# Key and value loads cut in two halves, and a new order of all engines, in a gated delta-rule attention kernel on one core

## The chip, the cores and the metric

The kernel runs on one core of a Trainium2 chip. Five engines work side by side, each through its own queue in order: PE (TensorE, matrix products into PSUM banks), DVE (VectorE), ACT (ScalarE), POOL (GpSimd), and SP (SyncE), which here issues every transfer (DMA). The metric is the device time of one execution in microseconds, lower is better. The time of before is the median of three runs.

## The reference

The input is four batches of eight heads, 768 tokens, 48 features per head. First a recurrence over tokens keeps a 48 x 48 state per head; then its output, 384 features per token, goes through a causal convolution gate and two products.

```python
def _attn_ref(q, k, v, beta):
    B, H, S, D = q.shape                       # 4, 8, 768, 48
    k_n = k / (np.linalg.norm(k, axis=-1, keepdims=True) + 1e-06)
    state = np.zeros((B, H, D, D), dtype=np.float32)
    for t in range(S):
        kt, vt, bt = (k_n[:, :, t], v[:, :, t], beta[:, :, t, None])
        y[:, :, t] = np.einsum('bhd,bhde->bhe', q[:, :, t], state)
        v_old = np.einsum('bhde,bhd->bhe', state, kt)
        state = state + bt[:, :, :, None] * np.einsum('bhd,bhe->bhde', kt, vt - v_old)
    return y

def _moe_ref(x, w_val, conv_w, w_out):         # x: (4, 768, 384)
    xp = np.concatenate([np.zeros((B, K - 1, D)), x], axis=1)
    for k in range(K):                         # K = 5
        gate_pre += conv_w[k][None, None, :] * xp[:, k:k + S, :]
    gate = 1.0 / (1.0 + np.exp(-gate_pre))
    return gate * (x @ w_val) @ w_out
```

## The kernel before

The 768 tokens are cut into twelve chunks of 64 (`ch` 0 to 11), two chunks to a group (`g` 0 to 5). All 32 head-and-batch pairs of a chunk lie in one tile in two halves of eight slots each (`h` 0 and 1, `HB` = 8).

Per group, `grams` loads keys by feature (`load_k`, tile KF, a part of KQ) and queries (`load_q`, tile R, also in KQ), multiplies keys with keys and queries (`kp`, `qp` in group 0, `kq` after it), and `prep` turns the key products into the coefficients of a triangular inverse. `prep` is a long row of small DVE steps: a transposition of GL into TLP (`trans_in`, L463), the norms and coefficients, rows and merges, then three transpositions out (`trans_out`, L520 and L523, the last writing XA). In every group but the first it begins with four small transfers inside GL (`realign`). Masked products go to KQ and AQ by DVE (L415).

Per chunk, `solve` finishes the inverse on PE with ACT between the steps: `m16` (out of XA), `m32` (YS), `lev1`, `lev2` (ZS), and six copies by ACT into XX. Then `chain` is the recurrence: `e` (state times keys), `eadd` on DVE (L631), `u` (XX times VT), six copies by ACT into Y and US, `s` (products with KT, keys by token, into the two banks SPS), four copies by ACT from SPS into the next chunk's Y (`sevac`), and so on to `e` of the next chunk. `y` gives the chunk's output, which ACT and twelve small transfers per group (X<-YSB) put in X. Chunk `ch` needs the state of chunk `ch - 1`, so this chain is serial over the chunks.

Per group, `moe` runs the convolution (ACT, then `tap` on DVE, L682), the sigmoid (`sig`, ACT, L686), the rounding of X into XH and XL, the products `val` (PE, L702), the gate (DVE, L707) and `outp` (PE, L712), and the stores. The weights are turned out of a 64-bit form on the way in by ACT, DVE and POOL (L299 to L318).

`Plan.add` records every step with what it reads and writes. The steps run in the order of a table of numbers, `ORDER`, which the program walks once; each engine then has its own steps in that order. `BANKS` says which of six PSUM banks a product takes. An entry of -1 in `ORDER` is `keep_warm` (L975): two matmuls of 128 x 128 zeros added to SPS, on PE alone, whose result changes nothing. Waits between engines and for transfers come from what the built instructions read and write. Transfers take eight semaphores in turn, and SP issues one only when the transfer eight places before it has landed.

Copies by ACT have line L228, the small products L243, transfers L233.

## Time and profile before

| | us |
|---|---|
| median of 3 runs | 310.89 (309.6 to 311.41) |
| the profiled execution, whole | 311.53 |
| its span, first to last instruction | 309.8 |
| PE busy | 276.2 |
| DVE busy | 230.5 |
| ACT busy | 205.7 |
| `keep_warm` on PE (L975) | 33.6 |

The span is what lies between the first and the last instruction; 1.7 us of the execution lie around it. A busy time is the sum over the span of the stretches in which the engine works on something. PE's busy time contains the `keep_warm` products, which are no work of the reference. The times of the rows further down run from the span's start.

### The profile page before, as it was taken

Reading aid. Unit: us, or ns where it says so; the run is one execution under the profiler, and the core shown is the slowest. Engines: PE = TensorE matmul, PEld = TensorE weight load, DVE = VectorE, ACT = ScalarE, POOL = GpSimd, SP = SyncE. Lnnn points to the kernel's source line nnn. Section 1 sums busy time; section 2 is a strip of 40 time slices with the busy share of each in tenths; the row PEclk is TensorE's granted clock in tenths of the full one; section 3 lists DMA queues with packets and bytes.
Section 4 is the critical chain, followed back from the end, with each engine's and each line's share of the span. In section 5 each row is a group of like instructions: output and inputs, shape, how many; then the busy total and the mean of one; then the engine's idle time right before and its main releaser. Section 6 shows DMA issues by size and latency. Waiting matters only on the chain.

```text
span 309.8 us, 15471 instructions
## 1 busy us (share of the span) xinstructions
PE 276.2 (89%) x6814; PEld 228.7 (74%) x6814; DVE 230.5 (74%) x560; ACT 205.7 (66%) x484; POOL 60.4 (19%) x111
## 2 busy tenths in 40 slices
PE   8566995989897699999899999998899999999994
PEld 4455984978786597778786868977587878796862
DVE  7899869267999468979797869995759988425570
ACT  2914636467968649759767778877478867975541
POOL 8511381050820000600005000040500060000000
PEclk9999798799999679999999999999699999999999
DMA  7999094074257325454573275146240532103222
GB/s 183 212 260 200 17 228 132 2 210 143 72 127 189 95 61 140 113 150 136 131 194 72 56 253 159 34 123 196 48 130 5 134 89 66 55 6 112 66 66 62
DMA packets 33155, 36.63 MB, mean 118 GB/s; under 512 B 18752, under 2 KB 25024, under 8 KB 33088
## 3 DMA queue, kind: packets, MB, share of 16 engines
q1 hardware_dynamic: 33088, 35.65, 43.9%
q8 instruction: 53, 0.87, 1.2%
q14 instruction: 14, 0.11, 0.1%
HBM read 22.92 MB, written 4.72 MB: 89 GB/s over the span
## 4 chain that ended last, share of the span: by engine, by line
PE 51%; DMA 13%; ACT 13%; DVE 11%; issue 6%; SPq 4%; ACTq 0%; DVEq 0%
PE PB L243 22%; PE PB L702 11%; PE PB L712 11%; PE SPS L975 5%; SPq L233 4%; DMA GT<-in_w_val_dram 4%; DMA X<-YSB 4%; ACT XX L228 3%; DMA KQ<-in_qr_dram 3%; DVE GT L682 2%; PE SPS L243 2%; DMA GT<-in_w_out_dram 2%; ACT G L228 2%; ACT Y L228 1%; DMA KQ<-AQ 1%
## 5 line engine op out<-in xcount | busy, mean ns | idle before, releaser
L682 DVE SCALAR_TENSOR_TENSOR GT<-X,CW,GT 128x512 f32<-128x512 f32 (+1 forms) x84 | 53.0, 669 | 8.5 <-ACT GT L228 8.2
L712 PE MATMUL PB<-WO,GT 128*128 128x384 f32 x144 | 53.1, 513 | 0.6 <-DVE GT L707 0.6
L228 ACT ACTIVATE XX<-PB 32x256 f32<-32x256 f32 (+2 forms) x96 | 39.6, 428 | 14.7 <-PE PB L243 11.5
L243 PE MATMUL PB<-KQ 48*64 48x128 f32 (+1 forms) x896 | 33.8, 301 | 9.7 <-issue 5.2
L712 PEld LDWEIGHTS PB<-WO,GT 128*128 128x128 f32 x144 | 26.7, 195 | 16.9 <-issue 1.4
L579 POOL TENSOR_TENSOR VT<-VT,NRM 128x768 f32<-128x768 f32 x12 | 21.1, 1766 | 90.1 <-PE PB L243 37.8
L243 PEld LDWEIGHTS PB<-KQ 48*64 48x64 f32 x896 | 28.2, 167 | 13.5 <-issue 8.9
L975 PE MATMUL SPS<-ZW 128*128 128x128 f32 x194 | 33.6, 326 | 3.0 <-ACT Y L228 2.7
L702 PE MATMUL PB<-XH,WVH 128*128 128x256 f32 x108 | 33.8, 313 | 0.3 <-ACT Y L228 0.2
L975 PEld LDWEIGHTS SPS<-ZW 128*128 128x128 f32 x194 | 28.5, 226 | 6.2 <-ACT Y L228 3.8
L702 PE MATMUL PB<-XL,WVH 128*128 128x256 f32 x108 | 31.0, 287 | 0.3 <-DVE XL L318 0.3
L702 PE MATMUL PB<-XH,WVL 128*128 128x256 f32 x108 | 30.9, 286 | 0.0
L228 ACT ACTIVATE GL<-PB 128x256 f32<-128x256 f32 (+1 forms) x44 | 16.4, 400 | 18.6 <-PE PB L243 17.4
L228 ACT ACTIVATE Y<-SPS 48x384 f32<-48x384 f32 (+1 forms) x44 | 20.7, 482 | 10.0 <-PE SPS L243 7.8
L707 DVE TENSOR_TENSOR GT<-PB,GT 128x256 f32<-128x256 f32 x36 | 14.6, 418 | 15.7 <-PE PB L702 7.9
L243 PE MATMUL PB<-KQ,Y 112*48 112x64 f32 (+2 forms) x768 | 25.3, 220 | 0.8 <-DVE GT L707 0.4
L243 PEld LDWEIGHTS PB<-KQ,Y 112*48 112x48 f32 (+2 forms) x768 | 22.5, 123 | 3.9 <-DVE KQ L415 1.0
L702 PEld LDWEIGHTS PB<-XH,WVH 128*128 128x128 f32 x108 | 21.0, 194 | 2.6 <-ACT Y L228 0.5
L230 POOL COPY W<-PR 32x256 f32<-32x256 f32 x24 | 9.4, 392 | 64.1 <-DVE PR L520 35.7
L702 PEld LDWEIGHTS PB<-XL,WVH 128*128 128x128 f32 x108 | 20.9, 194 | 0.7 <-DVE XL L318 0.7
L702 PEld LDWEIGHTS PB<-XH,WVL 128*128 128x128 f32 x108 | 21.0, 194 | 0.3
L415 DVE TENSOR_TENSOR KQ<-PB,MASK 64x256 f32<-64x256 f32 (+1 forms) x44 | 19.1, 442 | 2.6 <-PE PB L243 1.7
(101 smaller groups left out, 534.4 us busy)
## 6 DMA issues: line engine op xcount, KB each, us to landing
KQ<-in_kf_dram SPq DMA_DIRECT2D x12, 448.0 KB, 6.6
VT<-in_vt_dram SPq DMA_DIRECT2D x12, 384.0 KB, 5.2
KT<-in_kt_dram SPq DMA_DIRECT2D x12, 384.0 KB, 3.7
out_dram<-OS SPq DMA_DIRECT2D x20, 192.0 KB, 2.1
KQ<-in_qr_dram SPq DMA_DIRECT2D x12, 256.0 KB, 4.4
KQ<-AQ SPq DMA_DIRECT2D x24, 128.0 KB, 4.0
KQ<-in_qr_dram SPq DMA_DIRECT2D x12, 192.0 KB, 5.0
Y<-US SPq DMA_DIRECT2D x24, 96.0 KB, 3.0
```

The costliest lines, as they stand in the source:

```text
L228: A.activation(out=out, in_=in_, func=AF.Copy, **kw)
L230: eng.tensor_copy(out=out, in_=in_)
L233: SP.dma_start(out=dst, in_=src)
L243: PE.matmul(p, lhsT, rhs, start=start, stop=stop, tile_position=(row, col), skip_group_check=True)
L415: V.tensor_tensor(out=AQ[ch % NAQ][:, u:u + n] if v is None else R[ch % NR][r, v, u:u + n], in0=p[r], in1=MASK[h][r].unsqueeze(1).to_broad ...
L579: G.tensor_tensor(out=v, in0=v, in1=n.unsqueeze(3).to_broadcast([128, 2, HB, D]), op=ALU.mult)
L682: V.scalar_tensor_tensor(out=d, in0=XB[g % NX][:, m, :, t + k:t + k + n], scalar=CW[:, m, k:k + 1], in1=d, op0=ALU.mult, op1=ALU.add)
L702: PE.matmul(p[:, 0:n], w[:, k, 128 * m:128 * m + 128], v[:, n * k:n * k + n], start=j == 0, stop=j == len(ps_) - 1)
L707: V.tensor_tensor(out=d, in0=bank["val", ch, m][:, 0:B * C].rearrange("p (b t) -> p b t", t=C), in1=d, op=ALU.mult)
L712: PE.matmul(bank["out", g, t, i][:, 0:DM], gated(g, t, n)[:, k, nb * i:nb * i + nb].rearrange("p b t -> p (b t)"), WO[:, k, :], start=k == ...
L975: PE.matmul(SPS[0][:, 384:512], ZW, ZW, start=False, stop=True, skip_group_check=True)
```

## The change

The loads of keys by feature (KF), keys by token (KT) and values (VT) were one transfer each per chunk. Each is now two, one per half of the slots: 112 x 512 instead of 112 x 1024 floats for KF, 128 x 384 instead of 128 x 768 for KT and VT, and the plan has a token for each half. That makes 36 more transfers. The steps that read KF or KT wait for both halves' tokens in the plan; `vscale` on POOL still works on both halves of VT in one instruction.

The table `ORDER` has new numbers throughout (the numbers of the steps shift, since there are 36 more), and `BANKS` too. It has 71 entries of -1 instead of 97.

```diff
@@ -36,87 +36,89 @@
 ORDER = [
-    16, 1, 153, 31, 32, 34, 6, 36, 35, 0, 231, 33, 17, 232, 154, 12, 155, 7, 156, 30, 20, 18, 13, 37, 159, 151, 41,
...
+    16, 1, 157, 31, 32, 34, 20, 33, 36, 11, 237, 17, 38, 30, 158, 26, 163, 159, 0, 6, 35, 37, 18, 39, 2, 160, 235,
...
@@ -745,7 +747,9 @@
     def load_k(ch):
-        fetch(KF[ch % NKF][0:112], kf[ch], ch, [("KF", ch % NKF)], "LKF")
+        for h in range(2):
+            u = slice(HB * h, HB * h + HB)
+            fetch(KF[ch % NKF][0:112, u], kf[ch][:, u], ch, [("KF", ch % NKF, h)], "LKF")
@@ -756,7 +760,9 @@
     def load_kt(ch):
-        fetch(KT[ch % NKTB], kt[ch], ch, [("KT", ch % NKTB)], "LKT")
+        for h in range(2):
+            u = slice(HB * h, HB * h + HB)
+            fetch(KT[ch % NKTB][:, u], kt[ch][:, u], ch, [("KT", ch % NKTB, h)], "LKT")
@@ -788,7 +794,7 @@
-                add("PE", kq, (ch, i), r=[("KF", ch % NKF)] + q_of(ch), w=toks, take=toks)
+                add("PE", kq, (ch, i), r=[("KF", ch % NKF, h) for h in range(2)] + q_of(ch), w=toks, take=toks)
@@ -851,7 +857,9 @@
     def load_v(ch):
-        fetch(VT[ch % NVT], vt[ch], ch, [("VT", ch % NVT, h) for h in range(2)], "LV")
+        for h in range(2):
+            u = slice(HB * h, HB * h + HB)
+            fetch(VT[ch % NVT][:, u], vt[ch][:, u], ch, [("VT", ch % NVT, h)], "LV")
         add("POOL", vscale, (ch,), r=[("NRM", ch // 2 % 2)], w=[("VT", ch % NVT, h) for h in range(2)])
@@ -876,7 +884,7 @@
-            add("PE", s, (ch,), r=[("KT", ch % NKTB)] + us + [("U", h) for h in range(2)], w=[("SPS", x) for x in range(2)])
+            add("PE", s, (ch,), r=[("KT", ch % NKTB, h) for h in range(2)] + us + [("U", h) for h in range(2)], w=[("SPS", x) for x in range(2)])
```

The same change of tokens stands at `kp`, `qp` and `e`. Two lines more in the table shift every later line of the kernel: a row with L243 before has L245 after, L975 becomes L983.

Three places of the new order follow. The first is PE from the end of the wait before the first `m16` (XA, G) to the first `u` (VT, XX). The rows with ZW are `keep_warm`, YS is `m32`, XX with GL is `lev1`, ZS is `lev2`, KQ is `kq`. Before:

```order
211 L975 MATMUL SPS_115<-ZW 128x128 x18
212 L243 MATMUL PB_122<-XA,G_73 64x32 x16
213 L243 MATMUL PB_121<-XA,G_73 64x32 x16
214 L975 MATMUL SPS_115<-ZW 128x128 x3
215 L243 MATMUL PB_120<-YS,W_74 64x64 x16
```

```order
232 L243 MATMUL PB_120<-XX_75,GL_71 32x32 x32
233 L975 MATMUL SPS_115<-ZW 128x128 x3
234 L243 MATMUL PB_120<-ZS,XX_75 32x64 x32
235 L243 MATMUL PB_121<-YS,W_74 64x64 x16
236 L975 MATMUL SPS_115<-ZW 128x128 x9
237 L243 MATMUL PB_119<-VT_64,XX_75 64x48
```

After, first the same piece up to the `kq` that now follows `lev2`, then the end of the first `u` and what follows it:

```order
211 L245 MATMUL PB_119<-XA,G_73 64x32 x16
212 L983 MATMUL SPS_115<-ZW 128x128 x6
213 L245 MATMUL PB_117<-YS,W_74 64x64 x16
214 L245 MATMUL PB_119<-XA,G_73 64x32 x16
215 L245 MATMUL PB_122<-XX_75,GL_71 32x32 x32
216 L983 MATMUL SPS_115<-ZW 128x128 x3
217 L245 MATMUL PB_120<-ZS,XX_75 32x64 x32
218 L245 MATMUL PB_121<-KQ 64x128
```

```order
266 L245 MATMUL PB_119<-VT_64,XX_75 64x48
267 L245 MATMUL PB_120<-YS,W_74 64x64 x16
268 L983 MATMUL SPS_115<-ZW 128x128 x2
269 L245 MATMUL SPS_115<-Y_69,KT_62 48x48
270 L245 MATMUL SPS_116<-US,KT_62 48x48
```

The `m32` of chunk 1 stood between `lev2` and `u` of chunk 0, with nine `keep_warm` behind it; it now stands behind that `u`, and one `kq` and six `keep_warm` stand in its place. Further on, `m16` of chunks 2 and 3 and both halves of `kq` of chunk 5 now stand ahead of `e` of chunk 2; before, `m16` of both stood behind it.

The second place is ACT at the four copies of chunk 2's state product out of SPS into Y, and the first sigmoid with its table load. Before:

```order
124 L228 ACTIVATE G_73<-GL_71 16x32x16 x2
125 L228 ACTIVATE Y_70<-SPS_116 48x2x192
126 L686 ACT_TABLE_LOAD
127 L686 ACTIVATE GT_91<-GT_91 128x512
128 L228 ACTIVATE Y_70<-SPS_116 64x2x192
129 L228 ACTIVATE Y_70<-SPS_115 64x2x192
130 L228 ACTIVATE Y_70<-SPS_115 48x2x192
```

After:

```order
125 L230 ACTIVATE XH<-X_87 128x768
126 L230 ACTIVATE Y_70<-SPS_115 64x2x192
127 L230 ACTIVATE Y_70<-SPS_116 48x2x192
128 L230 ACTIVATE Y_70<-SPS_115 48x2x192
129 L230 ACTIVATE Y_70<-SPS_116 64x2x192
130 L688 ACT_TABLE_LOAD
131 L688 ACTIVATE GT_91<-GT_91 128x512
```

The table load and the sigmoid stood between the first and the second of the four copies; they now stand behind all four.

The third place is SP at the twelve transfers X<-YSB of group 0, up to the realigning transfers GL of group 2. Before:

```order
40 L233 DMA KT_63<-in_kt_dram 128x768
41 L233 DMA X_87<-YSB_89 16x4x64 x3
42 L233 DMA VT_64<-in_vt_dram 128x768
43 L233 DMA X_87<-YSB_89 16x4x64 x3
44 L233 DMA X_87<-YSB_90 16x4x64 x6
45 L233 DMA KT_62<-in_kt_dram 128x768
46 L233 DMA GL_71<-GL_71 32x16x32 x4
```

After:

```order
46 L235 DMA X_87<-YSB_89 16x4x64
47 L235 DMA VT_66<-in_vt_dram 128x384
48 L235 DMA X_87<-YSB_89 16x4x64
49 L235 DMA KQ<-in_kf_dram 112x512
50 L235 DMA X_87<-YSB_89 16x4x64 x2
51 L235 DMA KQ<-AQ_68 64x512
52 L235 DMA X_87<-YSB_89 16x4x64 x2
53 L235 DMA VT_65<-in_vt_dram 128x384
54 L235 DMA X_87<-YSB_90 16x4x64 x3
55 L235 DMA KQ<-in_qr_dram 48x1024
56 L235 DMA X_87<-YSB_90 16x4x64
57 L235 DMA GL_71<-GL_71 32x16x32 x4
```

Two more X transfers follow, with a query load between them. Between the first and the last of the twelve stood one other transfer; now ten do.

## Rows read from the trace of the kernel before

**Rows 1.** The page's head and its first part: the span, and the busy time of each engine with its share and its instructions.

```profile
span 309.8 us, 15471 instructions
PE 276.2 (89%) x6814; PEld 228.7 (74%) x6814; DVE 230.5 (74%) x560; ACT 205.7 (66%) x484; POOL 60.4 (19%) x111
```

**Rows 2.** The group of `keep_warm` on PE: busy us, mean ns of one, idle time before it.

```profile
L975 PE MATMUL SPS<-ZW 128*128 128x128 f32 x194 | 33.6, 326 | 3.0 <-ACT Y L228 2.7 <-issue 0.3
```

**Rows 3.** Busy time by stretch, all engines: length, then PE, PEld, DVE, ACT and POOL with their instructions, the granted clock, DMA share and GB/s.

```profile
13.15:39.28 26.13, 18.84 (x248) 16.95 (x249) 24.22 (x68) 11.42 (x25) 5.50 (x8) 0.93 0.71 169
43.98:82.38 38.40, 32.38 (x987) 28.91 (x982) 26.95 (x75) 26.42 (x66) 12.78 (x14) 0.91 0.44 132
80.00:305.50 225.50, 212.65 (x5350) 173.53 (x5348) 169.96 (x397) 161.19 (x383) 28.70 (x40) 0.96 0.39 105
```

**Rows 4.** The last of these stretches again, of `keep_warm` (L975) alone: length, PE and PEld, clock, DMA.

```profile
80.00:305.50 225.50, 9.48 (x50) 7.12 (x48) 0.96 0.39 105
```

**Rows 5.** DVE in order of time: start, us, line, operation, and the idle time before it with its releaser. The first `trans_in`, the last `trans_out` of group 0, the second `trans_in`, and the two long waits behind it (a step of the weights, then `eadd` of chunk 1).

```profile
13.15 1.95 DVE L463 STREAM_TRANSPOSE TLP<-GL 128x1024 f32<-128x1024 f32 x1
...
38.20 1.07 DVE L523 STREAM_TRANSPOSE XA<-TT__81 64x512 f32<-64x512 f32 x1
...
43.98 2.00 DVE L463 STREAM_TRANSPOSE TLP<-GL 128x1024 f32<-128x1024 f32 x1 [2.37 <-DMA GL<-GL]
...
60.33 0.36 DVE L301 TENSOR_SCALAR GT<-GT 128x384 f32<-128x384 f32 x1 [6.11 <-ACT GT L299]
...
66.90 1.02 DVE L631 TENSOR_TENSOR VT<-PB,VT 128x384 f32<-128x384 f32 x2 [2.88 <-PE PB L243]
```

**Rows 6.** PE in order of time, from the first `m16` to the first `u`.

```profile
40.24 2.06 PE L243 MATMUL PB<-XA,G 128*64 128x32 f32 x64 [0.29 <-DVE AQ L415]
42.23 0.94 PE L975 MATMUL SPS<-ZW 128*128 128x128 f32 x6
43.09 1.15 PE L243 MATMUL PB<-YS,W 128*64 128x64 f32 x32
44.17 1.10 PE L243 MATMUL PB<-KQ 48*64 48x128 f32 x32
...
46.99 1.10 PE L243 MATMUL PB<-ZS,XX 32*32 32x64 f32 x64
48.27 0.56 PE L243 MATMUL PB<-YS,W 128*64 128x64 f32 x10 [0.18 <-ACT YS L228]
52.32 1.54 PE L243 MATMUL PB<-YS,W 128*64 128x64 f32 x22 [3.49 <-issue]
53.80 4.21 PE L975 MATMUL SPS<-ZW 128*128 128x128 f32 x18
57.94 1.18 PE L243 MATMUL PB<-VT,XX 64*64 64x48 f32 x64
```

**Rows 7.** ACT in order of time: the last of the copies into XX of chunk 0's solution, then, at 102, the four copies of chunk 2's state product with the table load and the first sigmoid.

```profile
53.90 1.43 ACT L228 ACTIVATE XX<-PB 128x256 f32<-128x256 f32 x4 [2.50 <-PE PB L243]
...
102.37 0.48 ACT L228 ACTIVATE Y<-SPS 48x384 f32<-48x384 f32 x1 [2.51 <-PE SPS L243]
102.87 1.28 ACT L686 ACT_TABLE_LOAD   x1
104.17 0.63 ACT L686 ACTIVATE GT<-GT 128x512 f32<-128x512 f32 x1
104.82 0.86 ACT L228 ACTIVATE Y<-SPS 64x384 f32<-64x384 f32 x2
106.99 0.48 ACT L228 ACTIVATE Y<-SPS 48x384 f32<-48x384 f32 x1 [1.31 <-PE SPS L975]
```

**Rows 8.** PE in order of time: the `e` of chunk 2, the first `m16` of group 1, and the `e` of chunk 3.

```profile
81.23 1.14 PE L243 MATMUL PB<-Y,KQ 48*64 48x48 f32 x62 [0.85 <-ACT X L228]
...
83.17 1.12 PE L243 MATMUL PB<-XA,G 128*64 128x32 f32 x32
...
108.68 1.96 PE L243 MATMUL PB<-Y,KQ 48*64 48x48 f32 x64
```

**Rows 9.** Busy time by stretch, as in Rows 3, of a stall of PE, of the stretch behind it, and of a later stretch at the same clock.

```profile
48.80:52.30 3.50, 0.03 (x1) 0.00 (x0) 3.39 (x14) 2.53 (x5) 0.00 (x0) 0.85 0.28 96
51.20:58.00 6.80, 5.68 (x44) 5.34 (x45) 2.89 (x10) 1.60 (x5) 1.99 (x2) 0.50 0.01 2
102.40:112.70 10.30, 8.73 (x148) 7.65 (x141) 3.79 (x15) 7.54 (x14) 0.00 (x0) 0.50 0.34 95
```

**Rows 10.** DMA queues, packets, MB and share of the sixteen engines: the loads' queue from 45.9 to 49.9, and the queue that brings instructions from 48.8 to 52.3.

```profile
q1 hardware_dynamic: 425, 1.07, 89.9%
...
q8 instruction: 1, 0.02, 2.1%
```

**Rows 11.** SP in order of time: the twelve X transfers of group 0, in two runs with one load of VT between them.

```profile
74.58 1.97 SPq L233 DMA_DIRECT2D X<-YSB  x3
...
77.22 7.41 SPq L233 DMA_DIRECT2D X<-YSB  x9
```

**Rows 12.** DMA issues on the page, KB each and us to landing: the stores of two sizes; and the loads' queue over the first 26 us.

```profile
out_dram<-OS SPq DMA_DIRECT2D x20, 192.0 KB, 2.1
...
out_dram<-OS SPq DMA_DIRECT2D x8, 96.0 KB, 2.2
...
q1 hardware_dynamic: 2117, 5.67, 94.1%
```

More of the change, by code (lines that the diff above doesn't have):

```diff
@@ L38 @@
 ORDER = [
[76 rows of a table removed]
[78 rows of a table added]
 ]
 BANKS = (
-    "01231045533344432350152533302312133324430212541450451505430213320240311552045051103514425450234103220223421045"
-    "20515305214035353405243415122205013300321450435045023452240540152020154201224051251030153041235104445013435252"
-    "010542"
+    "01234510205323525032301431115254241035353434244154302040145000345450411545510541033340502525302513553445120440"
+    "34125154012241124434240315115032344551003134153054232413053445322324204510554312213125012512400503542015241343"
+    "534105"
 )
@@ L774, in grams @@
                 toks = [("kp", ch, h) for h in range(2)]
-                add("PE", kp, (ch,), r=[("KF", ch % NKF)], w=toks, take=toks)
+                add("PE", kp, (ch,), r=[("KF", ch % NKF, h) for h in range(2)], w=toks, take=toks)
                 for h in range(2):
@@ L782, in grams @@
                 toks = [("qp", ch, h) for h in range(2)]
-                add("PE", qp, (ch,), r=[("KF", ch % NKF)] + q_of(ch), w=toks, take=toks)
+                add("PE", qp, (ch,), r=[("KF", ch % NKF, h) for h in range(2)] + q_of(ch), w=toks, take=toks)
                 plan_att(att0, ch, toks, ())
@@ L864, in chain @@
             toks = [("e", ch, h) for h in range(2)]
-            add("PE", e, (ch,), r=[("KF", ch % NKF)] + [("Y", c2, "S", x, v) for x in range(2) for v in range(2)], w=toks, take=toks)
+            add("PE", e, (ch,), r=[("KF", ch % NKF, h) for h in range(2)] + [("Y", c2, "S", x, v) for x in range(2) for v in range(2)], w=toks, take=toks)
             for h in range(2):
```

152 rows, old and new, of the table ORDER are left out of this document.

## The prediction, made blind

> **What bounds the kernel now.** I read the page's first part, then the stretches, then PE, DVE and ACT in order of time through the first 110 us. PE is busy for 276.2 of 309.8 us [rows 1], but 33.6 us of that is `keep_warm`, so PE has some 243 us of real work, 34 us of filler and 34 us of idleness [rows 1, 2]. From 80 us on PE works through 212.65 of 225.5 us [rows 3], 9.48 of them filler [rows 4]: little more than its own work is left there. What can be won lies mostly ahead of 80 us, where PE waits for a serial path: DVE's `prep` of group 0 (24.22 busy of 26.13 us), then the first solution, and DVE's `prep` of group 1 (26.95 busy of 38.40) [rows 3]. So I price the early path, one place at 102 us, and what 36 more transfers cost on SP.
>
> The profiled execution took 311.5 us, 0.6 above the median of 310.9. I sum against 311.5 and take 0.6 off at the end.
>
> **The halves by themselves: 0.** The products take the two halves' slots in turn, so the second matmul of a group needs the second half; `vscale` needs both halves of VT. No reader starts earlier for having two tokens. What the halves allow is another order on SP. The first `prep` needs the same two whole KF loads first, and DVE has as much ahead of the first m16 as before: between the first transposition in and the last one out the order lists, beside the steps of `prep`, ten masked products and eight weight steps before, eleven and six now. I leave the first `m16` at 40.24 (bounds 2 us earlier to 1 us later).
>
> **First `m16` to first `u`: -5.7.** Before, this took from 40.24 to 57.94, 17.7 us [rows 6]. `lev2` ended at 48.09, but `m32` of chunk 1 stood next, stalled in its middle for 3.49 us with no releaser, and nine `keep_warm` behind it ran to 58.01, at half the clock (0.50 [rows 9], the lower of the levels of 1.2 and 2.4 GHz), though ACT's last copy into XX was done at 53.90 + 1.43 = 55.33 [rows 7]. In the new order PE has `m16` 1.03, six `keep_warm` 1.8 (three took 0.94 at the full clock), `m32` 1.1, `m16` 1.03, `lev1` with three `keep_warm` 1.7 (from 45.27 to 46.99), `lev2` 1.1, `kq` 1.1, six `keep_warm` 1.8 [rows 6]: 10.7 us; `u` overlaps its neighbours a little, so I take 10.3. Meanwhile ACT makes its six copies at about 0.36 each [rows 7], 2.2 us, under the last two items. That saves 7.4 us.
>
> What the stall is decides whether all of that stays. In the 4 us ahead of it the loads moved 1.07 MB at 89.9%, and within the stall one block of 16 KB came on the queue that brings instructions [rows 10]; I read it as PE waiting for instructions behind loads. The new order issues other loads there, but loads all the same, so I keep half of it: 1.7 us. First `u` at 52.2, 5.7 us earlier (bounds 3.9 to 7.4).
>
> The Trainium skill's page "Runtime: NRT & Kernel Launch", section "Instruction fetch mechanics", says that the sequencer fetches 256 instructions ahead on a DMA queue of its own and that this cost is mostly hidden. Here it is not: 3.49 us. By that page the stall would be something else that goes with the move of `m32`, and the result would be 1.7 us lower.
>
> **First `u` to `e` of chunk 2: +3.5.** `m16` of chunks 2 and 3 now stands ahead of this `e`, so `prep` of group 1 must be done.
> - Its transposition began at 43.98 after 2.37 us of waiting for the realigning transfers GL [rows 5], which by the order SP issued with query loads between them; now the four go in a row, so it begins at 41.6.
> - DVE then waited 6.11 us for a step of the weights, released at 60.33, 2.4 us after the first `u` began [rows 5, 6]. On ACT that step still stands behind `u`'s copies and now also behind two of `m32`: 52.2 + 2.4 + 0.8 = 55.4.
> - `eadd` of chunk 1 came at 66.90, 9.0 us after `u`: now 61.2. From there DVE took 15.5 us to the end of `prep` at 82.38 [rows 3, 5]. The new order puts 2.6 us less of DVE's work ahead of `eadd` (summed by the rows of the same steps), so 18.1 us follow: 79.3 instead of 82.38.
> - `m16` followed that by 0.8 us [rows 8]; now 80.1, and with two of them (2.2) `e` comes at 82.3, against 81.23: 1.1 us later. But 3.3 us of work are done by then that stood behind it (both `m16` and one more `kq`).
>
> Against before, by work done, that is -2.2. As `u` was 5.7 earlier, this part gives back 3.5. Bounds of the net: 0.9 later (if `prep` still ends at 82.38: 85.4 - 81.23 - 3.3) to 5 earlier (if `eadd` follows `u` by 7 us and the stall goes).
>
> **The table load at 102: -3.9.** `e` of chunk 3 waits for four copies out of SPS. The first ran at 102.37, then the table load 1.28 and a sigmoid 0.63, then the rest, the last ending at 107.47 after waiting for `keep_warm` (1.31) [rows 7]; `e` began at 108.68 [rows 8]. With the four in a row (4 x 0.48 = 1.9) `e` can begin about 2.5 us after 102.3, at 104.8: 3.9 earlier. The load moves behind them, ahead of the copies for chunk 3's `u`; PE has `e`, both `y` of chunk 2 and more there as cover, so I charge nothing (bounds -4.3 to -2).
>
> **The slow stretch there: -1.4.** From 102.4 to 112.7 the clock was 0.50, through these waits, and PE was busy 8.73 us [rows 9], 3.2 of them filler by my reading of the same stretch. The other 5.5 would be 2.7 faster at 1.00. I take half.
>
> **The rest of the filler: -2.6.** Of 9.48 us after 80 [rows 4] 3.2 are at this place; four `keep_warm` (1.1) stay. The other 5.2 were put where waits stood. They gain only if the waits go as well; I take half (bounds 0 to -5.2).
>
> **SP: +1.2.** In group 0 twelve X transfers took 9.4 us for twelve and one load, 0.6 to 0.8 each [rows 11]. Ten other transfers now stand among them instead of one, so the last X is 9 x 0.6 = 5.4 us later. Chunk 0's sixth has two more ahead of it: 1.2 us, on the path to `val`. The second six are covered by `m16`, `m32` and `e` on PE (bounds 0 to 5.4). Keys by token of chunk 11 are read by nobody; that half load stands among the last stores, 0 to 0.5 us; I take 0.
>
> **Sum:** -2.2 - 3.9 - 1.4 - 2.6 + 1.2 = -8.9; 311.5 - 8.9 - 0.6 = 302.0.
>
> **Rivals.**
> - *Waits stay where filler was* (0.14). `prep` of group 1 ends no sooner (+0.9), the slow stretch and the other waits stay (0): 0.9 - 3.9 + 1.2 = -1.8, so 309 to 311. For it: DVE and not PE ends last in group 1, and fewer `keep_warm` may just turn filler into idleness. Against it: at `u` the filler itself was late by 2.6 us.
> - *SP becomes the bound* (0.11), slower. SP is in order, and everything behind a waiting transfer waits: X, then the rounding into XH and XL, then `val`. If the last X is 5.4 us later in three groups with PE out of other work, that is 16.2 on top of -10.1: 317. It decides from the third such group on. For it: SP already issued nine X back to back [rows 11]. Against it: from 120 us on PE has `outp` and `val` of the group before to fill with.
> - *Each transfer pays a fixed price* (0.04), slower. Stores of 192 and 96 KB both land in about 2.1 us [rows 12], so a half costs as much as a whole when alone; six more among the first loads at 2.1 each would start everything 12.6 us later: 314.6. Against it: through the first 26 us the queue was busy for 94.1% [rows 12], so the fixed part lay beside other transfers. The Trainium skill's page "DMA: Bandwidth & Descriptors", section "Bandwidth", says to batch transfers to 1 MiB or more since each carries some 2 us; it speaks for this rival, and the busy share speaks against it here.
> - *The stalls for instructions go* (0.15). Smaller loads queue less ahead of an instruction block. The 3.49 us (1.7 more here), its like later on, and low stretches such as the 10.3 us at 0.50 [rows 9] would go, some 3 us for each of two: 293 to 297. They may also only move.
>
> **Chances.** The forecast has 0.56, its own range 298 to 307. Faster by over 0.5% (1.6 us, about what a measurement of this kernel can tell from no change): 0.56, 0.15 and 0.02 of the first rival, 0.73. Within 0.5%: 0.12. Slower: 0.15. The range 295.5 to 312 leaves out the two slower rivals and a little of the last.
>
> **What would show it.** First `u` near 52 and not near 58; the second transposition in on DVE near 41.6; `prep` of group 1 ending by 80; four copies out of SPS in a row before the table load, and `e` of chunk 3 within 3 us of the `s` before it. The forecast is wrong if `u` stays near 58, if a stall over 3 us with no releaser stands ahead of it, or if X on ACT or DVE is a longer wait than before.

## The result and the profile after

The changed kernel took 300.85 us (median of four runs, 298.94 to 302.63) against 310.53 for the kernel before (four runs beside it). The ratio is 0.9688 with a 95% interval of 0.9617 to 0.9758: faster, by 9.7 us. The profiled execution took 302.63 us, 8.90 less than before's 311.53, and 1.73 of it lie around the span in both. Of the runs further down a time is the median of all executions, while a ratio compares only the fast ones (within 1.5% of the fastest of that kernel) with the fast ones of before, so the two can differ by about 1%; for `m32` put later in the old order and for the table load put first in the new one a ratio rests on two executions, for the kernel without filler on three.

The head of the page of after, its first part, and in the second fence the group of `keep_warm` (busy us, mean ns of one, idle time before it):

```profile
span 300.9 us, 15436 instructions
PE 266.2 (88%) x6762; PEld 220.0 (73%) x6762; DVE 234.4 (78%) x560; ACT 206.4 (69%) x484; POOL 58.1 (19%) x111
```

```profile
L983 PE MATMUL SPS<-ZW 128*128 128x128 f32 x142 | 23.9, 325 | 2.3 <-ACT Y L230 2.3
```

PE is busy 10.0 us less than in [rows 1], and `keep_warm` is 9.7 us less than in [rows 2]. So PE's real work is as long as before, 242 us, in a span that is 8.9 shorter, and PE is idle for 34.7 us where it was for 33.6: what has gone from the span is filler, and the idle time did not grow in its place. Of the filler that is left, 1.42 us lie behind 80 us, where [rows 4] had 9.48. This is the stretch from 80 us on, of `keep_warm` alone (length, PE, PEld, clock, DMA):

```profile
80.00:300.90 220.90, 1.42 (x8) 1.04 (x8) 0.98 0.41 108
```

PE of after in order of time: the first `m16`, a stall in `lev1`, and the first `u`; then `m16` of chunks 2 and 3, `e` of chunk 2, and the first part of `e` of chunk 3:

```profile
38.66 1.12 PE L245 MATMUL PB<-XA,G 128*64 128x32 f32 x32 [0.49 <-DVE X L242]
...
44.87 0.26 PE L245 MATMUL PB<-XX,GL 32*32 32x32 f32 x8 [0.95 <-issue]
...
49.97 1.41 PE L245 MATMUL PB<-VT,XX 64*64 64x48 f32 x64 [0.38 <-issue]
...
79.07 2.06 PE L245 MATMUL PB<-XA,G 128*64 128x32 f32 x64
81.06 1.29 PE L245 MATMUL PB<-Y,KQ 48*64 48x48 f32 x64
...
100.52 0.78 PE L245 MATMUL PB<-Y,KQ 48*64 48x48 f32 x35
```

Set against [rows 6, 8], the starts of the same steps cut both executions into stretches; for `e` of chunk 2 in before that is the start of its 62 products, as in the prediction (its first two ran at 80.07). `m16` of chunks 2 and 3 (2.06) and one `kq` (1.10) now stand ahead of `e` of chunk 2, which moves 3.2 us of work from the fourth stretch into the third. One `val` of chunk 1 (nine products, 1.2 us) now stands behind `e` of chunk 3 and not ahead of it, which moves 1.2 us from the fourth into the last. The third column is before's program in a second execution (the run with the empty edit, below).

| stretch on PE | before | before again | after | after less before | without the moved work | the sum had |
|---|---|---|---|---|---|---|
| start to first `m16` | 40.24 | 42.89 | 38.66 | -1.6 | -1.6 | 0 |
| to first `u` | 17.70 | 14.54 | 11.31 | -6.4 | -6.4 | -5.7 |
| to `e` of chunk 2 | 23.29 | 23.59 | 31.09 | +7.8 | +4.6 | +3.5 |
| to `e` of chunk 3 | 27.45 | 25.11 | 19.46 | -8.0 | -3.6 | -3.9 - 1.4 |
| to the end of the span | 201.12 | 203.27 | 200.38 | -0.7 | -1.9 | -2.6 + 1.2 |
| sum | 309.80 | 309.40 | 300.90 | -8.9 | -8.9 | -8.9 |

The two executions of one program differ by 2.2 to 3.2 us in four of the five stretches, and by 0.4 in the whole. So a term of this table is known to some 3 us, and no better.

DVE of after in order of time, the rows that answer to [rows 5]: the second transposition in, the weight step and `eadd` of chunk 1 with the waits ahead of them, and the last transposition out of group 1:

```profile
41.66 1.98 DVE L465 STREAM_TRANSPOSE TLP<-GL 128x1024 f32<-128x1024 f32 x1
...
50.47 0.36 DVE L303 TENSOR_SCALAR GT<-GT 128x384 f32<-128x384 f32 x1 [2.50 <-ACT GT L301]
...
60.82 1.02 DVE L633 TENSOR_TENSOR VT<-PB,VT 128x384 f32<-128x384 f32 x2 [3.35 <-PE PB L245]
...
76.79 2.13 DVE L525 STREAM_TRANSPOSE XA<-TT__81 64x512 f32<-64x512 f32 x2
```

The second transposition began 2.3 us earlier than in [rows 5] and had no wait ahead of it, and `prep` of group 1 ended at 78.92 instead of 82.38.

ACT of after, the rows that answer to the second half of [rows 7]: all four copies out of SPS in one row, then the table load (the first sigmoid follows it):

```profile
98.24 1.86 ACT L230 ACTIVATE Y<-SPS 64x384 f32<-64x384 f32 x4 [0.29 <-PE SPS L245]
100.12 1.28 ACT L688 ACT_TABLE_LOAD   x1
```

Busy time by stretch, with the columns of [rows 9]: a new long stretch at the lower clock early on, and the stretch that was at 0.50 before:

```profile
12.10:29.00 16.90, 13.03 (x236) 11.75 (x236) 15.86 (x50) 7.50 (x18) 0.00 (x0) 0.50 1.06 221
...
102.40:112.70 10.30, 9.63 (x252) 8.63 (x255) 8.72 (x32) 7.75 (x21) 0.00 (x0) 1.00 0.51 129
```

### The profile page after: what moved, and what is told of

Same layout as the page of the kernel before. It is cut to its first block, busy times and chain, and to the rows that moved or that the text cites. A ratio compares the mean times of both kernels' runs of the same rounds, so it can differ in the third digit from the quotient of the medians.

```text
span 300.9 us, 15436 instructions
## 1 busy us (share of the span) xinstructions
PE 266.2 (88%) x6762; PEld 220.0 (73%) x6762; DVE 234.4 (78%) x560; ACT 206.4 (69%) x484; POOL 58.1 (19%) x111
## 4 chain that ended last, share of the span: by engine, by line
PE 41%; ACT 20%; DVE 12%; issue 9%; DMA 9%; SPq 3%; POOL 3%; POOLq 0%; DVEq 0%; ACTq 0%
PE PB L245 21%; PE PB L704 8%; PE PB L714 7%; ACT XX L230 5%; ACT Y L230 4%; SPq L235 3%; PE SPS L983 3%; DMA X<-YSB 3%; DMA KQ<-AQ 3%; ACT G L230 2%; PE SPS L245 2%; DVE GT L684 2%; ACT GT L688 2%; DMA out_dram<-OS 2%; DVE PR L511 1%
## 5 line engine op out<-in xcount | busy, mean ns | idle before, releaser
L684 DVE SCALAR_TENSOR_TENSOR GT<-X,CW,GT 128x512 f32<-128x512 f32 (+1 forms) x84 | 55.7, 683 | 9.4 <-ACT GT L230 8.9
L714 PE MATMUL PB<-WO,GT 128*128 128x384 f32 x144 | 51.4, 497 | 0.6 <-ACT XX L230 0.4
L245 PE MATMUL PB<-KQ 48*64 48x128 f32 (+1 forms) x896 | 33.0, 289 | 11.7 <-DMA KQ<-in_qr_dram 4.6
L245 PEld LDWEIGHTS PB<-KQ 48*64 48x64 f32 x896 | 27.5, 155 | 15.6 <-DMA KQ<-in_qr_dram 4.7
L714 PEld LDWEIGHTS PB<-WO,GT 128*128 128x128 f32 x144 | 25.7, 189 | 16.2 <-DVE AQ L417 0.8
L704 PE MATMUL PB<-XH,WVH 128*128 128x256 f32 x108 | 34.7, 321 | 0.0
L581 POOL TENSOR_TENSOR VT<-VT,NRM 128x768 f32<-128x768 f32 x12 | 19.3, 1614 | 39.6 <-DVE TT__81 L517 30.9
L245 PE MATMUL PB<-KQ,Y 112*48 112x64 f32 (+2 forms) x768 | 26.0, 221 | 1.0 <-ACT Y L230 0.5
L983 PE MATMUL SPS<-ZW 128*128 128x128 f32 x142 | 23.9, 325 | 2.3 <-ACT Y L230 2.3
L245 PEld LDWEIGHTS PB<-KQ,Y 112*48 112x48 f32 (+2 forms) x768 | 22.9, 123 | 3.5 <-ACT Y L230 0.7
L983 PEld LDWEIGHTS SPS<-ZW 128*128 128x128 f32 x142 | 21.0, 230 | 4.1 <-ACT Y L230 2.7
L230 ACT ACTIVATE Y<-SPS 64x384 f32<-64x384 f32 (+1 forms) x44 | 20.6, 482 | 3.6 <-PE SPS L245 2.7
```

The source lines that it names most:

```text
L230: A.activation(out=out, in_=in_, func=AF.Copy, **kw)
L245: PE.matmul(p, lhsT, rhs, start=start, stop=stop, tile_position=(row, col), skip_group_check=True)
L581: G.tensor_tensor(out=v, in0=v, in1=n.unsqueeze(3).to_broadcast([128, 2, HB, D]), op=ALU.mult)
L684: V.scalar_tensor_tensor(out=d, in0=XB[g % NX][:, m, :, t + k:t + k + n], scalar=CW[:, m, k:k + 1], in1=d, op0=ALU.mult, op1=ALU.add)
L704: PE.matmul(p[:, 0:n], w[:, k, 128 * m:128 * m + 128], v[:, n * k:n * k + n], start=j == 0, stop=j == len(ps_) - 1)
L714: PE.matmul(bank["out", g, t, i][:, 0:DM], gated(g, t, n)[:, k, nb * i:nb * i + nb].rearrange("p b t -> p (b t)"), WO[:, k, :], start=k == ...
```

## The experiments

By the table every term came within 1.7 us of the forecast, which is closer than one pair of executions can show. Whether its reasons are the causes is another question. The theory: the gain lies in the two places that the sum prices, the way to the first `u` and the table load at 102 us. The rivals: it lies in the halves, in the late filler, or in no single place. A ratio is always to executions of the kernel before beside it; before itself took between 304.4 and 315.3 us in these, so an edit worth less than about 2 us is not resolved.

**The halves alone, and the new order without them.** In the first, every KF, KT and VT load of before is two transfers issued back to back; in the second, the loads of after are whole again, each where its first half stood. ORDER of before, where the first two loads of KF become four (the other numbers shift):

```diff
-16, 1, 153, 31, 32, 34, 6, 36, 35, 0,
+16, 1, 157, 31, 32, 33, 34, 36, 6, 38, 37, 0,
```

> The kernel before with every KF, KT and VT load cut in two halves issued one behind the other, in the old order. My theory (the halves by themselves are worth nothing): 309.5 to 311.5. Rival one (each transfer pays a fixed price on SP or on the queue): 312.5 to 316. Rival two (smaller loads let instruction blocks through, and that is where the gain comes from): stalls of PE with no releaser shrink, 303 to 307.

Measured: 309.66 us, ratio 0.9974 (0.9916 to 1.0032). No effect can be told.

ORDER of after, where the first four halves become two loads again:

```diff
-16, 1, 157, 31, 32, 34, 20, 33, 36, 11,
+16, 1, 153, 31, 32, 20, 34, 11,
```

> The new order with the loads of KF, KT and VT whole again, each where its first half stood. My theory (the halves allow an order on SP, and carry little by themselves): 0 to 3 us above after, that is 6.5 to 9.5 us below before; instruction blocks behind the bigger loads may cost some stalls of 1 to 2 us. Rival (the halves carry the gain): within 3 us of before.

Measured: 301.28 us, ratio 0.9659 (0.9609 to 0.9709), the same as after. The halves carry nothing that can be measured, neither a gain nor a price; what counts is the order, with the banks that belong to it.

**The first `u`, both ways.** In the old order `m32` of chunk 1 and its copies go behind the first `u`, `lev1` of chunk 1 behind the first `s`, and the nine `keep_warm` go away; in the new order they are put back. PE in the old order:

```diff
 L243 MATMUL PB_120<-ZS,XX_75 32x64 x32
+L243 MATMUL PB_119<-VT_64,XX_75 64x48
...
 L243 MATMUL PB_121<-YS,W_74 64x64 x16
-L975 MATMUL SPS_115<-ZW 128x128 x9
-L243 MATMUL PB_119<-VT_64,XX_75 64x48
```

> The kernel before with one edit of the order: m32 of chunk 1 (and ACT's two copies behind it) moves behind the first u, lev1 of chunk 1 behind the first s, and the nine keep_warm ahead of the first u are dropped. My theory (these two stood in the way of the first u, and about half of what u wins is given back because DVE's prep of group 1 follows at its own pace): first u at 51 to 53 instead of 57.94, e of chunk 1 some 5 us earlier than 65.58, e of chunk 2 1 to 3 us earlier than 80.07, time 306.5 to 309 against 310.5 for before. Rival (the early path does not set the end; what counts lies after 100 us): u earlier all the same, but the time within 1 us of before.

Measured: 315.47 us, ratio 1.012 (1.0046 to 1.0195): nothing won, if anything slower. PE in order of time (`u` but for its first two products, `e` of chunk 1, and `m16` of chunk 2), then `e` of chunk 1 in before, then DVE's wait for `eadd` of chunk 1:

```profile
52.72 1.48 PE L243 MATMUL PB<-VT,XX 64*64 64x48 f32 x62 [0.41 <-ACT XX L228]
...
64.83 1.15 PE L243 MATMUL PB<-Y,KQ 48*64 48x48 f32 x64
...
82.53 1.12 PE L243 MATMUL PB<-XA,G 128*64 128x32 f32 x32
```

```profile
65.58 1.15 PE L243 MATMUL PB<-Y,KQ 48*64 48x48 f32 x64
```

```profile
66.14 1.02 DVE L631 TENSOR_TENSOR VT<-PB,VT 128x384 f32<-128x384 f32 x2 [6.74 <-PE PB L243]
```

`u` came 5.2 us earlier, as forecast, and `m16` of chunk 2 only 0.6. Most of the lead was gone before DVE could use it: the first `s` came 3.4 us earlier (58.11 against 61.49), and `e` of chunk 1 only 0.75, not the 5 expected. On PE `m32`, `keep_warm`, `lev1` and `lev2` of chunk 1 stand between, with a stall of 1.23 us in `lev2`, and the last copy out of SPS waited 1.52 for `keep_warm`. DVE no longer waited 6.11 for the weight step; it waited 6.74 for that `e` instead, and `eadd` began at 66.14 against 66.90 in [rows 5]. Why the time rose stays open: the four executions took from 311.99 (the profiled one) to 318.32.

In the new order, PE:

```diff
 L245 MATMUL PB_117<-KQ 64x128
-L983 MATMUL SPS_115<-ZW 128x128 x6
...
+L245 MATMUL PB_122<-YS,W_74 64x64 x16
+L983 MATMUL SPS_115<-ZW 128x128 x9
...
-L245 MATMUL PB_120<-YS,W_74 64x64 x16
 L983 MATMUL SPS_115<-ZW 128x128 x2
```

> The kernel after with m32 of chunk 1, its two copies on ACT and nine keep_warm put back ahead of the first u. By the prediction's second step the first u would be 3 to 5 us later than 49.97 and the time 2 to 4 us above after. By what the same edit of the old order showed (first u 5.9 us earlier, m16 of chunk 2 only 0.6, no gain): u 2 to 5 us later, m16 of chunk 2 within 1.5 us of 79.07, time within 2 us of after.

Measured: 302.37 us, ratio 0.9748 (0.9666 to 0.9831); it overlaps that of after. The first `u` began at 51.39, 1.4 us later, `e` of chunk 1 at 59.20 as in after (59.21), and `m16` of chunk 2 at 78.34, 0.7 earlier. That is less at `u` than either line had expected, since `m32` and nine `keep_warm` took 3.4 us here where they took 9.7 with the stall and the low clock in [rows 6].

```profile
47.99 1.26 PE L245 MATMUL PB<-YS,W 128*64 128x64 f32 x32
...
51.39 1.15 PE L245 MATMUL PB<-VT,XX 64*64 64x48 f32 x64
```

**The table load, both ways.** ACT in the old order, and in the new:

```diff
 L228 ACTIVATE Y_70<-SPS_116 48x2x192
+L228 ACTIVATE Y_70<-SPS_116 64x2x192
+L228 ACTIVATE Y_70<-SPS_115 64x2x192
+L228 ACTIVATE Y_70<-SPS_115 48x2x192
 L686 ACT_TABLE_LOAD
 L686 ACTIVATE GT_91<-GT_91 128x512
-L228 ACTIVATE Y_70<-SPS_116 64x2x192
-L228 ACTIVATE Y_70<-SPS_115 64x2x192
-L228 ACTIVATE Y_70<-SPS_115 48x2x192
...
 L230 ACTIVATE Y_70<-SPS_115 64x2x192
-L230 ACTIVATE Y_70<-SPS_116 48x2x192
-L230 ACTIVATE Y_70<-SPS_115 48x2x192
-L230 ACTIVATE Y_70<-SPS_116 64x2x192
 L688 ACT_TABLE_LOAD
 L688 ACTIVATE GT_91<-GT_91 128x512
+L230 ACTIVATE Y_70<-SPS_116 48x2x192
+L230 ACTIVATE Y_70<-SPS_115 48x2x192
+L230 ACTIVATE Y_70<-SPS_116 64x2x192
```

> The kernel before with one edit of the order: the first sigmoid of group 0, which brings its table load, moves behind the fourth copy out of SPS on ACT. My theory (the 3.9 us of the sum): e of chunk 3 at 104.5 to 106.5 instead of 108.68, since the keep_warm between the copies still hold the last one back a little, and the time 307 to 309. Rival (the load only moves into the copies of the next solution, so u of chunk 3 is as late as before): e earlier, u of chunk 3 still at 113 to 114, time 310 to 311.

Measured: 309.45 us, ratio 1.0038 (0.9951 to 1.0124). ACT and then PE (all but the first two products of `e` of chunk 3, and `u` of chunk 3) in order of time:

```profile
100.80 0.98 ACT L228 ACTIVATE Y<-SPS 48x384 f32<-48x384 f32 x2 [2.42 <-PE SPS L243]
...
103.48 0.49 ACT L228 ACTIVATE Y<-SPS 48x384 f32<-48x384 f32 x1 [0.80 <-PE SPS L975]
103.99 1.28 ACT L686 ACT_TABLE_LOAD   x1
```

```profile
106.42 1.92 PE L243 MATMUL PB<-Y,KQ 48*64 48x48 f32 x62 [1.45 <-DVE GT L707]
...
112.41 1.55 PE L243 MATMUL PB<-VT,XX 64*64 64x48 f32 x64
```

> The kernel after with the first sigmoid and so its table load put back between the first and the second of the four copies out of SPS for chunk 3. By the sum of the prediction: e of chunk 3 some 2 to 4 us later than in after (102.4 to 104.5 instead of 100.52), and the time 2 to 4 us above after, 5.5 to 7.5 below before. Rival, as in the old order (the load only changes places with the copies of the next solution): e later, u of chunk 3 at 104.9 to 106.5, time within 1.5 us of after.

Measured: 302.43 us, ratio 0.9651 (0.9579 to 0.9723): by the ratio not slower than after, by the medians 1.6 us above it.

In the old order the copies did come together, and `e` had another wait behind them (1.45, the gate on DVE). Counted from the first copy, `u` of chunk 3 came after 11.6 us (100.80 to 112.41), in before after 11.5 (102.37 to 113.84): what `e` won, `u` did not keep. Between the two PE worked through two `val` at the lower clock (0.50 from 108.3 to 112.4 us) without a wait, and the load and the sigmoid stood ahead of the XX copies. So the rival that was put on record holds there, as far as `u` goes; that the copies are what held `u` is not shown, since the last ended 2.5 us ahead of it. In the new order the load between the copies is felt on the spot: from the first copy (96.19) to `e` it took 4.9 us (101.13) instead of 2.3, and to `u` 10.0 (106.21) instead of 6.7. In the time a cost of up to some 2 us can't be told from none. The 3.9 us of the sum are a distance in one trace, and no price of that instruction.

**Two loads behind the first `u`: an empty edit.** ORDER had them moved so:

```diff
-275, 340, 276, 138, 277, 131, 384, 278,
+275, 276, 138, 277, 131, 278,
...
-343, 287,
+343, 340, 384, 287,
```

> The kernel before with two loads (KT of chunk 1 and VT of chunk 2, 393 KB each) issued behind the first u instead of at 42.8 and 44.5 us. If the stall of 3.49 us in m32 of chunk 1 is PE waiting for a block of instructions behind loads, the block has 0.3 to 0.6 MB ahead of it instead of 1.07: stall 0.5 to 2 us, first u at 55 to 56.5, time 308 to 310. If it is something that goes with m32 itself: stall still above 3 us, u at 57.5 to 58.5, time 310 to 311.5.

SP has no other transfer between the two places, so each engine's stream is that of the kernel before, word for word, and this is the kernel before a second time: 308.14 us, ratio 1.0028 (0.9974 to 1.0081). As a test of the loads it says nothing. It shows something else, in PE's order of time (the first `m16`, `lev1` of chunk 0, `m32` of chunk 1, the first `u` but for two products, `e` of chunk 2 likewise, `e` of chunk 3):

```profile
42.89 2.06 PE L243 MATMUL PB<-XA,G 128*64 128x32 f32 x64
...
49.60 0.62 PE L243 MATMUL PB<-XX,GL 32*32 32x32 f32 x48 [1.42 <-issue]
...
52.95 1.74 PE L243 MATMUL PB<-YS,W 128*64 128x64 f32 x32
...
57.43 1.14 PE L243 MATMUL PB<-VT,XX 64*64 64x48 f32 x62 [0.29 <-ACT XX L228]
...
81.02 1.14 PE L243 MATMUL PB<-Y,KQ 48*64 48x48 f32 x62 [0.66 <-ACT X L228]
...
106.13 1.96 PE L243 MATMUL PB<-Y,KQ 48*64 48x48 f32 x64
```

The same program that had stalled for 3.49 us within `m32` of chunk 1 [rows 6] now ran `m32` through, and stalled for 1.42 in `lev1` of chunk 0, an earlier place of the stream. So the stall is no property of `m32`, though three other kernels with this piece of the old order have it there too (2.45, 3.21 and 2.33 us). In both executions one block came on the queue that brings instructions, and the stall ended 2.2 to 2.4 us after that block began to move: at 49.9 in before, at 47.3 here. In the 2.7 us ahead of the block the loads' queue moved 0.93 MB at a share of 91.6%:

```profile
q1 hardware_dynamic: 340, 0.93, 91.6%
```

That fits PE waiting for instructions behind loads, as [rows 10] did (its 4 us end where the block began, 1.1 us into the stall); a kernel that really issues these loads elsewhere was not tried, so it is argued and not shown.

**Where the order wins.** Three kernels take one order up to a step and the other order for all steps that are left. The cut is `e` of chunk 4 (near 125 us) in two of them, and `e` of chunk 2 (near 81 us) in the third. A few products take another bank. ORDER behind the cut, against after, at `e` of chunk 4 (836):

```diff
-836, 573, 570, 748, 663, 574, 749,
+836, 636, 959, 831, 750, 639, 570,
```

and at `e` of chunk 2 (592):

```diff
-592, 324, 333, 722, 226, 444, 425,
+592, 395, 587, 588, -1, 422, -1,
```

> Halves, the new order up to and with e of chunk 4 and, of the steps that are left, the old order (one product in another bank). The three edits of the old order told that no single place holds the gain, but after has u of chunk 3 8.9 us earlier than before and keeps that to the end. My theory (the gain is made by the new order of the first 125 us as a whole: both solutions of group 1 done ahead of the chain, the table load behind the copies, fewer loads beside instruction blocks): e of chunk 4 at 123 to 124.5 as in after, time 4 to 9 us below before. Rival (the late filler, 9.48 us after 80 us, is what the change wins): within 2 us of before.

Measured: 304.45 us, ratio 0.9823 (0.9766 to 0.9881): about 5.5 of the 9.7 us. The start of `e` of chunk 4 in before, in after and in this kernel:

```profile
127.98 1.15 PE L243 MATMUL PB<-Y,KQ 48*64 48x48 f32 x64
```

```profile
123.33 1.26 PE L245 MATMUL PB<-Y,KQ 48*64 48x48 f32 x64
```

```profile
120.86 1.57 PE L245 MATMUL PB<-Y,KQ 48*64 48x48 f32 x64
```

At the cut after is 4.65 us ahead of before, with one more `m16` done (1.1), and not the 8 to 10 that the expectations read; the rest of its 8.9 comes behind it. The cut kernel is 2.5 us ahead of after there. At `e` of chunk 6 it is still 2.9 ahead (163.95 against 166.80, where after has 0.8 us more work done), at `e` of chunk 9 it is 4.2 behind (228.29 against 224.12, where after has 2.3 us less done). So the old tail falls behind between these two.

> Halves, the old order up to and with e of chunk 4 and the new order of the rest (three products in another bank). My theory: within 2 us of before, at most 3 us below, since from 125 us on before and after take about as long (the gain stands between 8 and 10 us all through that stretch). Rival (late filler): 4 to 9 us below before.

Measured: 309.63 us, ratio 1.0058 (1.0020 to 1.0096): nothing won. This kernel has no `keep_warm` behind `e` of chunk 4, where before has 4.0 us of it, so leaving that part of the late filler out is worth nothing by itself. The other 5.3 us of it, between `e` of chunks 2 and 3, were not left out alone.

> Halves, the new order up to and with e of chunk 2 and, of the steps that are left, the old order (five products in other banks). With the cut at e of chunk 4 the time was 5 us below before. My theory (by then the gain is made: DVE's prep of group 1 began sooner and waited less, and both m16 of group 1 are done): 3 to 6 us below before, m16 of chunk 3 at 78.5 to 81.5, u of chunk 3 well below 110. Rival one (the order from 82 to 125 us, with the table load and the solution of chunk 3 ahead of e of chunk 3, is where the gain is made): within 1.5 us of before. Rival two (each half gives a part): 1.5 to 3 us below.

Measured: 310.61 us, ratio 1.0052 (1.0009 to 1.0095): nothing won, though both `m16` of group 1 began at 78.14 and so 5 to 6 us ahead of before. By `lev1` of chunk 2 that lead was down to 0.2 (88.84 against 89.08). ACT and then PE in order of time in this kernel, `m16` and `lev1` of chunk 2:

```profile
87.39 0.72 ACT L230 ACTIVATE GT<-X,CW 128x512 f32<-128x512 f32 x1 [4.56 <-DMA X<-YSB]
88.13 0.66 ACT L230 ACTIVATE XX<-PB 128x256 f32<-128x256 f32 x2
```

```profile
78.14 2.06 PE L245 MATMUL PB<-XA,G 128*64 128x32 f32 x64
...
88.84 1.07 PE L245 MATMUL PB<-XX,GL 32*32 32x32 f32 x64 [3.95 <-ACT XX L230]
```

The same place on ACT in after:

```profile
84.65 0.66 ACT L230 ACTIVATE XX<-PB 128x256 f32<-128x256 f32 x2 [0.56 <-PE PB L245]
...
88.59 0.72 ACT L230 ACTIVATE GT<-X,CW 128x512 f32<-128x512 f32 x1 [1.11 <-DMA X<-YSB]
```

And SP's last X transfer of this group in after:

```profile
85.08 1.42 SPq L235 DMA_DIRECT2D X<-YSB  x1
```

This wait is where most of the lead went. The convolution takes X in three parts. The new SP order sends the third part last, and the new ACT order takes it last, behind the copies of the next solution, with a wait of 1.11. The old ACT order, made for an SP that sends the twelve nearly in a row [rows 11], takes the third part ahead of those copies. Behind the new SP it stands for 4.56 us there, and `lev1` on PE behind it for 3.95. The seam has a share in it, since the new head had already run the part that the old order keeps for last. Here, then, ACT's order and SP's don't fit each other; that this is what decides everywhere is argued from this place and the two cuts, and not shown.

**DVE's waits taken out of the new order.** A try to beat both kernels: what made DVE wait within `prep` of group 1 is put behind steps of `prep`. DVE, one of the places:

```diff
 L489 TENSOR_TENSOR PR_82<-TT__81,TLP 128x64
-L633 TENSOR_TENSOR VT_65<-PB_120,VT_65 128x384
-L633 TENSOR_TENSOR VT_65<-PB_122,VT_65 128x384
 L492 TENSOR_REDUCE TT__81<-PR_82 128x4x4
...
 L489 TENSOR_TENSOR PR_82<-TT__81,TLP 128x144
+L633 TENSOR_TENSOR VT_65<-PB_120,VT_65 128x384
+L633 TENSOR_TENSOR VT_65<-PB_122,VT_65 128x384
```

> The kernel after with DVE's prep of group 1 put ahead of what made it wait: four weight steps some eight small steps later, eadd of chunk 1 behind seven steps of prep instead of three, three masked products behind the last rows, five later weight steps behind the last transposition out (on PE one kq thereby stands ahead of the second u). DVE waited 2.50, 3.35, 1.27 and 0.97 us at these places in after. My theory as the runs have left it (not the first u but the end of this prep, and with it m16 of chunk 2, sets what follows): m16 of chunk 2 at 73 to 76.5 instead of 79.07, u of chunk 2 3 to 5 us earlier than 91.32, time 3 to 5 us below after, 12 to 15 below before. Rival (from 80 us on PE has no room, 203.6 busy of 220.9 us, so something else ends last at once): m16 earlier, the time within 1.5 us of after.

Measured: 302.75 us, ratio 0.9808 (0.9732 to 0.9883); no gain. DVE's last transposition out, and PE's steps from the two `kq` on (`m16`, and later `m32`):

```profile
74.65 2.12 DVE L525 STREAM_TRANSPOSE XA<-TT__81 64x512 f32<-64x512 f32 x2
```

```profile
77.41 1.98 PE L245 MATMUL PB<-KQ 48*64 48x128 f32 x64
...
80.62 2.06 PE L245 MATMUL PB<-XA,G 128*64 128x32 f32 x64
...
86.01 1.15 PE L245 MATMUL PB<-YS,W 128*64 128x64 f32 x32 [2.02 <-POOL W L232]
```

`prep` ended at 76.77, 2.2 us earlier than in after, and `m16` began 1.6 us later: two `kq` and five `keep_warm` stand ahead of it on PE, as in after, and here PE came to them 1.7 us later (77.41 against 75.71). From 64 to 71 us PE's granted clock was 0.51 here and 1.00 in after. Behind `m16`, `m32` waits for a copy on POOL (2.02). Neither line of the expectation held; with the wait gone from DVE, PE came last.

**No filler.** After without its 71 `keep_warm`:

```diff
-241, 63, 347, 99, -1, 262, 102, 14, 168, -1, 103, -1, 245,
+241, 63, 347, 99, 262, 102, 14, 168, 103, 245,
```

> The kernel after without any keep_warm (71 of them left out, which change nothing in the result; 67 stand in the first 80 us). Theory one (they fill waits that DVE and the loads cause, and cost nothing): within 1.5 us of after, the same stretches at the lower clock. Theory two (they hold the clock): more stretches at 0.50 and 3 to 8 us more. Theory three (they are late themselves, as the nine ahead of the first u were in the old order): 2 to 4 us less.

Measured: 304.97 us, ratio 0.9802 (0.9707 to 0.9898). Its six runs had a mean granted clock of 0.869 to 0.911, the four of after 0.941 to 0.960. From 38.66 to 86.10 us, first here (in the longest of the six runs), then in after:

```profile
38.66:86.10 47.44, 37.24 (x1076) 34.56 (x1080) 34.22 (x89) 32.84 (x79) 20.18 (x26) 0.64 0.48 130
```

```profile
38.66:86.10 47.44, 41.21 (x1240) 37.34 (x1244) 36.74 (x89) 33.80 (x82) 22.48 (x27) 0.96 0.48 127
```

The filler does hold the clock: without it the clock of this stretch is 0.64 on average instead of 0.96. In time that is worth little here: the intervals of the two ratios overlap, so the gain of keeping it lies between nothing and some 9 us, and at 4 by the medians, which is nearest to the second theory.

## Why the prediction was right, and where its reasons were not

The forecast was 302.0 and the time 300.85; against the profiled execution the sum of -8.9 is what was measured, -8.90. That it agrees to a tenth is luck. The terms missed by -1.6, -0.7, +1.1, +1.7 and -0.5, which cancel, and before's second execution would have moved single terms by up to 3.2 us. What was right is the direction and the size of the whole. Point by point:

- **The halves: 0.** Right, shown from both sides (0.9974, and 0.9659 for the new order without them). With that the rival of a fixed price for each transfer falls: 36 more of them cost nothing that shows. The Trainium skill's page "DMA: Bandwidth & Descriptors", section "Bandwidth", which asks for transfers of 1 MiB or more, spoke for that rival. Whole loads (384 and 448 KB) and halves (192 and 224 KB) both lie below that size, so the runs don't test the rule itself; within it, halving the size has no price here that shows.
- **First `m16` unmoved.** It came 1.6 us earlier, within the bounds. In before's second execution it came 2.65 later, and the whole took no longer for it.
- **To the first `u`: -5.7.** -6.4 measured. Half of the stall was kept in the sum; 0.95 us of stall stood there (within `lev1`), with 0.38 ahead of `u`. Right in size. As a cause it failed: done alone in the old order it brought `u` 5.2 us forward and won no time (1.012); undone in the new order it moved `u` by only 1.4 us.
- **Given back until `e` of chunk 2: +3.5.** +4.6 measured. The second transposition was forecast at 41.6 and came at 41.66, `eadd` at 61.2 and came at 60.82, the end of `prep` at 79.3 and came at 78.92, `m16` at 80.1 and came at 79.07. That the lead at `u` is mostly given back was right, and the edit in the old order shows it too (0.6 of 5.2 us left at `m16`). That DVE's order alone sets `m16` is not shown: in that edit the lead was lost on PE before `e` of chunk 1, and with `prep` ended 2.2 us earlier in the new order `m16` still came later.
- **The table load: -3.9.** The four copies stood in a row, and `e` of chunk 3 began 2.3 us after the copies did, as forecast (6.3 in before). But what the step claimed, that this instruction's place is worth 3.9 us of the time, failed: moved alone in the old order it won nothing (1.0038), and put back in the new one it costs at most some 2 us.
- **The slow stretch: -1.4.** It is gone (1.00 from 102.4 to 112.7). Together with the step before, -5.3 were forecast and -3.6 measured; the two can't be told apart. And 2.4 of these 3.6 have no term in the sum: before stalled in this stretch with no releaser for 2.01 us in `s` of chunk 2 and 0.61 ahead of `u`, after for 0.26. The first of them:

```profile
101.44 0.20 PE L243 MATMUL SPS<-Y,KT 64*48 64x48 f32 x1 [2.01 <-issue]
```

- **The rest of the filler and SP: -2.6 + 1.2.** -1.9 measured, in place of -1.4. Of the late filler that went, the part behind `e` of chunk 4 is worth nothing by itself (1.0058); for the rest that is open. On SP the last X of group 0 was issued at 85.08, 1.0 us later than in before (84.04) and not 5.4, because the first of them left 6 us earlier (68.23 instead of 74.58). But a sign that the prediction named as speaking against it did come: the convolution on ACT waited longer for X than before (us in total, times, longest; before, then after). So the step was right that X comes later to its reader; the time was reached in spite of it.

```profile
ACT GT L228 <- DMA X<-YSB: 5.1, 5, 1.5
```

```profile
ACT GT L230 <- DMA X<-YSB: 9.3, 8, 2.0
```

- **The rival that stalls for instructions go.** In part. This is PE's idle time with no releaser on its small products (us in total, times, longest), of before, of after, of the new order with whole loads, and of the kernel cut at `e` of chunk 2:

```profile
PE PB L243 <- issue: 12.3, 8, 3.5
```

```profile
PE PB L245 <- issue: 8.4, 13, 1.5
```

```profile
PE PB L243 <- issue: 11.2, 11, 2.2
```

```profile
PE PB L245 <- issue: 6.3, 9, 1.5
```

With the products into SPS that makes 15.5 us in before, 8.9 in after, 12.5 with whole loads and 7.2 in the cut kernel. After does stall less than before. But the cut kernel stalls least and is not faster than before, so less stalling alone does not bring the gain; and the new order with whole loads stalls 3.6 us more than after and takes no longer. The Trainium skill's page "Runtime: NRT & Kernel Launch", section "Instruction fetch mechanics", calls the cost of fetching mostly hidden; if these stalls are fetches, the traces do not agree for stretches in which loads back up.

So the sum got the whole about right by following the new order through one trace, stretch by stretch, where all engines move at once. Where it spoke of single edits as if each carried its term, it was wrong: no single edit tried, in the old order or the new, moved the time by its term. Nor do the two parts of the order add up: the new head alone won 1.8%, the new tail alone nothing, both together 3.1%.

Which part of the new order wins is settled by the cuts as far as they go: nothing up to 81 us alone, 1.8% up to 125 us, the rest only with the tail. Why the parts need each other was seen at one place (ACT's wait of 4.56 us) and stays open beyond it.

## What to carry to other kernels

In a kernel whose engines all run a written order, a step brought forward is worth what the other engines' orders let through behind it; follow it to the next serial step on each engine before giving it a price. Take the trace of one program twice before giving a stretch of it a price: here two executions of the same length differed by up to 3.2 us in one stretch. Test an order by cutting it, new up to a step and old from there on, rather than by moving single instructions, and look in the cut kernel for the wait that appears. And look at each engine's own stream after an edit of a common table: an edit there may move nothing at all.

## What was not expected

- The same program stalls in different places. PE's stall with no releaser was 3.49 us in `m32` of chunk 1 in one execution and 1.42 us in `lev1` of chunk 0 in another; the two took 311.53 and 311.12 us.
- The longest stretch at the lower clock cost nothing that shows: after ran at 0.50 (1.2 GHz) from 12.1 to 29.0 us, while DVE was busy for 15.86 of 16.90 us, and its first `m16` still came 1.6 us earlier than before's.
- Without filler the mean granted clock fell by some 0.06, and the time by the medians rose only 4 us.
